# Attention on one core: q's shifted projection is turned in place of its features, and key sums and gate products are issued as four column quarters

## Chip, core and metric

One core of one Trainium2 chip. The metric is device time in microseconds (us) for one launch. The engines are TensorE (PE, with its weight loads shown apart as PEld), VectorE (DVE), ScalarE (ACT), GpSimd (POOL) and SyncE (SP), which works off its instructions beside the others; each does its own in the order in which they stand.

## The reference

Linear attention with an exponential feature map, then two top-1 mixtures of experts on its rows. Shapes: 8 batches, 8 heads, 576 rows, head dimension 64, 128 projected features; 4608 rows of 512 for the experts, 8 experts with a hidden size of 1024. The change touches the attention and the first gate alone:

```python
def phi(x):
    proj = np.einsum('bhsd,df->bhsf', x, w_phi)
    proj = proj - np.max(np.abs(proj), axis=-1, keepdims=True)
    return np.concatenate([np.exp(proj), np.exp(-proj)], axis=-1)
q_p, k_p = (phi(q), phi(k))
kv = np.einsum('bhsf,bhsd->bhfd', k_p, v)
z = np.sum(k_p, axis=2)
num = np.einsum('bhsf,bhfd->bhsd', q_p, kv)
den = np.einsum('bhsf,bhf->bhs', q_p, z)[..., None] + 1e-06
...
logits = x @ w_gate
```

A row's 256 features are thus two halves, exp(d) and exp(-d), of the same shifted projection d (128 values). `den` needs the key sums `z`; `logits` are the gate products, taken for the gate and the output gate together.

## The kernel before

The attention works through 32 heads: four groups (pairs of batches), eight heads each. A head has 2 x 576 rows in nine tiles of 128: eight whole ones and a last one that holds the 64 left-over rows of either batch. For a head the program makes the features of k and q, and in between finishes the head before it (`prev`):

- `turn` (L559) transposes k, q and the left-over tile on TensorE (L563) and splits them into high and low parts (ACT L567, DVE L568).
- `phi` (L571) makes the projection with three products per pair of tiles (L580 to L582, bank `pj`), takes the largest magnitude (DVE L584), subtracts it (DVE L585, tile `d`), and writes both halves with two exponentials (ACT L589, L590).
- `sums` (L604) forms k's features times v, one batch in either column half of the array (L611), copied to SBUF by ACT (L613). `total` (L593) adds k's features over the tiles on GpSimd into `fs` (L597 to L602).
- `turn_q` (L628) transposes q's features: 16 transposes (L635) for the eight tiles, copied by ACT and DVE in turn (L637), and two more (L640, copy L641) for the last one. The result `qt` has the features on partitions.
- `turn_sums` (L615) transposes the products (L620) and sums `fs` over its 128 partitions: four products whose weights are a 128 x 128 piece of `fs` and whose moving operand is one column of ones (L623). DVE copies both (L625, L626).
- `rows_out` (L644) multiplies `qt` with them (L653, L659, bank `nm`) and divides (L663 to L665).

After the eighth head of a group, `finish` (L669) stores the rows and makes three steps, each of which has the gate products of three tiles (`logits`, L499): per chunk of 128 features three transposes (L508), a copy (L510), and one product whose 32 columns of weights fill a quarter of the output partitions (L511, bank `lt`); a copy (L514) and a second product (L516) add the quarters. The last step also routes the 1152 rows (`route`, L111: a chain of small DVE operations, two rank products, L162 and L163, and nine scatters on GpSimd, L184). `next_part` (L709) takes one such step at two places of each following head.

```python
lt = ps.tile([P, 512], F32, tag=tag, name="lt", bufs=2)[:, :nt * P]
for kc in range(KC):
    tp = ps.tile([P, 4, P], F32, tag="tp", name="tp", bufs=3)[:, :nt, :]
    ...
    nc.tensor.matmul(lt[kc * GW:(kc + 1) * GW, :], gates[:, kc, :],
                     xt.rearrange("p t c -> p (t c)"), start=True, stop=True)
```

PSUM banks are rings: `tp` has three (all transposes), `pj` three, `nm` two (`kvt`, `kv`, `nm`, `lg`, `lt`, `rk`). In the attention the order on each engine is set by a scheduler when the program is built, not by the order of the text; the experts keep the order of the text. The experts (L307 on) run from about 546 us to the end.

Of the kernel before, what the change touches and what calls it, by code (L numbers as in the profile page):

```python
"""Linear attention with an exponential feature map, then two top-1 mixtures of experts.

Layout of the work
- Attention: per pair of batches and head, the 2 x 576 rows are nine tiles of 128 rows: four of each
  batch, and one whose halves are the last 64 rows of either batch. Scores, key sums and outputs
  stay on chip; the rows of x go to DRAM once.
- Routing: logits, first maximum, gate, and a row's rank among its expert's rows (a product with a
  strictly triangular matrix). A row's id and gate are scattered into a table [rank % 128, expert,
  rank / 128]; entries that no row takes keep the id of a row of zeros.
- Experts: an expert's weights are loaded and split once; its rows are gathered in blocks of 256 (or  # L10
  128 for a short rest), as many as its count asks for. Products run as float32r passes
  over exact high and low parts (high*high, high*low, low*high).
"""
# [17 lines left out]
P = 128  # L31
B, H, S, DH = 8, 8, 576, 64
N, D, F, E = B * S, H * DH, 1024, 8
NF = 128
# [9 lines left out]
class Fused:  # L44
# [8 lines left out]
    def consts(self):  # L53
# [5 lines left out]
        # upper[i, j] = 1 where i < j  # L59
# [7 lines left out]
        # E, E-1, .. 1: the first maximum has the largest  # L67
        self.rev = const.tile([P, E], F32, name="rev")
        nc.vector.tensor_copy(self.rev, iota_e)
        # [GW * c + e, e] = 1  # L70
# [5 lines left out]
        # the table in use; ids of the rows that wait to be routed  # L76
# [21 lines left out]
    def clear_steps(self, pool, *parts):  # L98
        """Steps that zero the rows of a routing from one on, so that others can be gathered before
        these are there."""  # L100
# [10 lines left out]
    def route(self, r, lg, nt, ids, padded=False):  # L111
        """lg: SBUF [P, nt, E or 2E] logits (and output-gate logits); ids: SBUF [P, nt] int32;
        padded: ids of N stand for no row. Returns what is left to do once PSUM for ranks is at hand:
        that in turn returns the scatters into the table."""
# [7 lines left out]
        # first maximum  # L122
# [5 lines left out]
        if padded:  # L128
            # no expert, and an address outside the table
            out = sm.tile([P, NT], F32, tag="out", name="out")[:, :nt]  # L130
            nc.vector.tensor_scalar(out, ids, float(N), float(1 << 20), op0=ALU.is_ge, op1=ALU.mult)
            nc.vector.tensor_tensor(w, w, out, op=ALU.add)
        oh = sm.tile([P, NT, E], F16, tag="oh", name="oh", bufs=3)[:, :nt, :]
        nc.vector.tensor_tensor(oh, rev, w.unsqueeze(2).to_broadcast([P, nt, E]), op=ALU.is_equal)
        # rows before, by expert
# [6 lines left out]
        # gate  # L142
# [17 lines left out]
        def place(rk):  # L160
            # rank among the expert's rows
# [12 lines left out]
            # (rank % P) * E * SLOTS + rank / P  # L174
# [15 lines left out]
    def early(self, r, psum):  # L190
        """The first expert's first block, of the rows routed so far: later rows take the blocks
        after it."""
# [12 lines left out]
    def end_route(self, r, psum):  # L205
        """Counts of rows by expert, and the table, on chip."""
# [13 lines left out]
    def start_stream(self, seq):  # L220
        """Weights of the experts of seq (w1, w2, e) in turn: loaded by chunks of 128 contraction
        rows, half an expert ahead of the split into high and low parts."""
# [17 lines left out]
    def split_steps(self, i):  # L240
        """Eight steps that leave the weights of expert i of the stream split."""
# [19 lines left out]
    def expert_buffers(self, pool):  # L261
        """Buffers of fixed place: what one branch leaves in them, another reads."""
# [17 lines left out]
    def place(self, r, e, c):  # L280
        """Table columns of rows c*256 .. (c+1)*256 of expert e: [P, 2, (id, scale)]."""
# [12 lines left out]
    def turn(self, i, k, ps, bufs=2):  # L294
        """Gathered rows i, transposed and split into x k."""
# [224 lines left out]
    def attention(self, q, k, v, w_phi, r, pool, ps, aside):  # L520
# [192 lines left out]
        for i in range(n_heads + 1):  # L713
# [16 lines left out]
            if prev:  # L730
                turn_q(prev)
            if prev:
                turn_sums(prev)
# [69 lines left out]
```

## Time and profile before

| | |
|---|---|
| median of 3 runs | 1633.69 us (1633.20 to 1636.33) |
| profiled execution, span from first to last instruction | 1630.8 us |
| between that span and the median | 2.9 us |
| TensorE busy | 1545.3 us, 95% of the span |
| VectorE, ScalarE, GpSimd busy | 48%, 38%, 26% |
| mean granted TensorE clock | 0.969 of full speed |

The profiled execution gives its span alone; what lies around it (start and end of a launch) is taken as the 2.9 us by which the median is above it. Busy time on TensorE overlaps from one product to the next, since ends are modelled. The chain of waits is therefore the better view of what a stretch costs there: its pieces follow each other without overlap.

### The profile page before, as it was taken

How to read it: one execution, taken by the hardware profiler on the slowest of the kernel's cores; microseconds unless marked ns; L12 is line 12 of the kernel's file. 1: busy time of each engine (PE TensorE's matmuls, PEld its weight loads, DVE VectorE, ACT ScalarE, POOL GpSimd, SP SyncE). 2: the span in 40 equal slices, each digit the busy share in tenths (PEclk: the TensorE clock that was granted, in tenths of full speed). 3: DMA queues.
4: the chain of work that ended last, by engine and by line, in shares of the span. 5: the costliest groups of instructions: out<-in, count | busy, mean ns of one | idle time of the engine just before them, and what ended most of it. 6: DMA issues, size and time to landing. Idle time of an engine off the chain costs nothing.

```text
span 1630.8 us, 28157 instructions
## 1 busy us (share of the span) xinstructions
PE 1545.3 (95%) x10958; PEld 1368.2 (84%) x10958; DVE 781.7 (48%) x2003; ACT 622.3 (38%) x1147; POOL 420.9 (26%) x433
## 2 busy tenths in 40 slices
PE   7999999999999989899899999998998989998997
PEld 6887897898788679798788898987998979897996
DVE  6776776676676535262545255324143244131410
ACT  5564454455454424242344244213244234131411
POOL 3332432443253321221221222214111212101100
PEclk9999899899999999999999999999999999999998
DMA  6764222123201422240433242305133344122200
GB/s 209 243 220 142 58 74 103 45 59 115 61 16 40 144 94 80 89 156 26 145 117 114 82 144 84 103 16 186 40 112 123 104 148 161 40 80 82 97 25 28
DMA packets 99089, 163.19 MB, mean 100 GB/s; under 512 B 25819, under 2 KB 62043, under 8 KB 97760
## 3 DMA queue, kind: packets, MB, share of 16 engines
q1 hardware_dynamic: 83008, 117.98, 22.1%
q0 software_dynamic: 15776, 41.52, 7.4%
q8 instruction: 146, 2.39, 0.6%
q14 instruction: 159, 1.30, 0.2%
HBM read 118.67 MB, written 42.88 MB: 99 GB/s over the span
## 4 chain that ended last, share of the span: by engine, by line
PE 59%; issue 19%; DMA 16%; POOL 2%; DVE 2%; ACT 1%; another core or an unknown queue 0%; POOLq 0%; SPq 0%; ACTq 0%
PE nm L653 7%; DMA out_dram<-y,tab 6%; DMA xg<-r_rows,tab 6%; PE kvt L611 5%; PE hp L328 5%; PE hp L330 4%; PE hp L329 4%; PE yp L353 4%; PE yp L355 4%; PE yp L354 4%; PE tp L635 3%; DMA r_table<-pay,at 3%; PE pj L580 3%; PE pj L582 2%; PE pj L581 2%
## 5 line engine op out<-in xcount | busy, mean ns | idle before, releaser
L346 DVE SCALAR_TENSOR_TENSOR hl<-hp,hh 128x512 fp32r<-128x512 f32 x148 | 102.1, 690 | 335.9 <-ACT hh L345 335.9
L345 ACT ACTIVATE hh<-hp 128x512 fp32r<-128x512 f32 x148 | 88.4, 597 | 270.0 <-PE hp L330 251.7
L359 ACT ACTIVATE y<-yp,tab 128x512 f32<-128x512 f32 x76 | 52.3, 689 | 290.3 <-PE yp L355 225.7
L184 POOL DMA_INDIRECT r_table<-pay,at x78 | 78.5, 1007 | 263.7 <-DVE at L180 222.3
L360 POOL DMA_INDIRECT out_dram<-y,tab x38 | 38.2, 1005 | 403.5 <-ACT y L359 402.0
L653 PE MATMUL nm<-kvs,qt 128*128 128x65 f32 x1024 | 123.7, 280 | 1.7 <-DVE kvs L626 1.7
L653 PEld LDWEIGHTS nm<-kvs,qt 128*128 128x128 f32 x1024 | 122.0, 198 | 3.1 <-PE tp L563 2.3
L584 DVE TENSOR_REDUCE am<-pj 128x4 f32<-128x512 f32 (+1 forms) x160 | 100.1, 633 | 43.1 <-PE pj L582 41.2
L589 ACT ACTIVATE phi<-d 128x1024 f32<-128x1024 f32 (+1 forms) x96 | 80.8, 842 | 52.4 <-DVE d L585 42.8
L597 POOL TENSOR_TENSOR fs<-phi 128x512 f32<-128x512 f32 x32 | 40.8, 1276 | 223.0 <-ACT phi L590 125.0
L580 PE MATMUL pj<-wh,th 128*128 128x256 f32 x288 | 91.5, 321 | 7.0 <-DVE pre L140 4.8
L585 DVE TENSOR_TENSOR d<-pj,am 128x512 f32<-128x512 f32 (+1 forms) x160 | 96.3, 628 | 0.3
L289 POOL DMA_INDIRECT xg<-r_rows,tab x82 | 84.5, 1030 | 38.1 <-issue 24.1
L383 DVE COPY xt<-tp 128x512 f32<-128x512 f32 x21 | 14.5, 692 | 156.2 <-PE tp L381 156.2
L360 POOL DMA_INDIRECT r_rows<-y,tab x38 | 37.6, 989 | 189.0 <-ACT y L359 179.7
L581 PE MATMUL pj<-wl,th 128*128 128x256 f32 x288 | 84.8, 297 | 0.0
L582 PE MATMUL pj<-wh,tl 128*128 128x256 f32 x288 | 83.1, 300 | 0.0
L599 POOL TENSOR_TENSOR fs<-fs,phi 128x512 f32<-128x512 f32 x64 | 81.3, 1270 | 5.0
L590 ACT ACTIVATE phi<-d 128x1024 f32<-128x1024 f32 (+1 forms) x96 | 79.8, 831 | 0.0
L580 PEld LDWEIGHTS pj<-wh,th 128*128 128x128 f32 x288 | 57.0, 198 | 17.2 <-issue 12.4
L635 PE MATMUL tp<-ident,phi 128*128 128x128 f32 x512 | 70.4, 274 | 0.1
L304 DVE TENSOR_TENSOR x<-tp,x 128x512 fp32r<-128x512 f32 x86 | 55.2, 682 | 25.4 <-ACT x L303 25.4
(294 smaller groups left out, 4759.4 us busy)
## 6 DMA issues: line engine op xcount, KB each, us to landing
raw<-in_moe_w_dram SPq DMA_DIRECT2D x128, 512.0 KB, 4.4
r_rows<-zero SPq DMA_DIRECT2D x15, 768.0 KB, 6.7
km<-in_k_dram SPq DMA_DIRECT2D x32, 256.0 KB, 2.9
qm<-in_q_dram SPq DMA_DIRECT2D x32, 256.0 KB, 3.5
vm<-in_v_dram SPq DMA_DIRECT2D x32, 256.0 KB, 3.2
r_rows<-x SPq DMA_DIRECT2D x8, 1024.0 KB, 5.5
xg<-r_rows,tab POOLq DMA_INDIRECT x82, 5.9
r_table<-pay,at POOLq DMA_INDIRECT x78, 2.2
```

Of the source, the lines that this page charges most:

```text
L289: self.nc.gpsimd.indirect_dma_start(self.xg[i][t][:, :], None, r["rows"], bass.IndirectOffsetOnAxis(ap=self.place(r, e, c)[:, t, 0:1], axi ...
L328: nc.tensor.matmul(o, w1h[kc][:, fs], x[:, kc, 0, :], start=first, stop=False)
L345: nc.scalar.activation(oh, hp, AF.Relu)
L346: nc.vector.scalar_tensor_tensor(ol, hp, 0.0, oh.bitcast(F32), op0=ALU.max, op1=ALU.subtract)
L580: nc.tensor.matmul(o, hi[:, i + j, :], wh, start=True, stop=False)
L581: nc.tensor.matmul(o, hi[:, i + j, :], wl, start=False, stop=False)
L582: nc.tensor.matmul(o, lo[:, i + j, :], wh, start=False, stop=True)
L584: nc.vector.tensor_reduce(am, pj, axis=AX.X, op=ALU.max, apply_absolute_value=True)
L585: nc.vector.tensor_tensor(d[:, 2 * i:2 * i + 2 * m, :], pj, am.unsqueeze(2).to_broadcast([P, 2 * m, NF]), op=ALU.subtract)
L611: nc.tensor.matmul(kvt[64 * b:64 * b + 64, :], v, f, start=(t == 0), stop=(t == 4))
L635: nc.tensor.transpose(tp[:, t, :], u["fq"][:, 4 * b + t, s * NF:(s + 1) * NF], self.ident)
L653: nc.tensor.matmul(nm[:, t, :], qt[:, s, 4 * b + t, :], kv[:, 2 * b + s, :], start=(s == 0), stop=(s == 1))
```

## The change

q's shifted projection `d` itself is transposed (nine transposes a head) and the two exponentials are taken by ScalarE from PSUM straight into `qt`; q's features are never written, save in the left-over tile's half for k. `key_sums` is new: four products with 32 columns of ones as weights and 128 columns of `fs` moving, each into its quarter of the partitions, a copy (`zt`) and one transpose. `logits` is parted: `turn_x` does twelve transposes with three copies 512 wide (before: four copies 384 wide), and the four gate products stand one after another. A group now leaves six steps in place of three, and `next_part` is called at three places of a head.

```diff
+    def turn_x(self, x, nt, ps, pool):
+        nc = self.nc
+        xt = pool.tile([P, KC * nt, P], F32, tag="xt", name="xt", bufs=1)
+        n = KC * nt
+        for j in range(0, n, 4):
+            tp = ps.tile([P, 4, P], F32, tag="tp", name="tp", bufs=3)
+            for i in range(j, j + 4):
+                kc, t = divmod(i, nt)
+                nc.tensor.transpose(tp[:, i - j, :], x[:, t, kc * P:(kc + 1) * P], self.ident)
+            (nc.scalar.copy if j % 8 else nc.vector.tensor_copy)(xt[:, j:j + 4, :], tp)
+        return xt
...
         for kc in range(KC):
-            tp = ps.tile([P, 4, P], F32, tag="tp", name="tp", bufs=3)[:, :nt, :]
-            for i in range(nt):
-                nc.tensor.transpose(tp[:, i, :], x[:, i, kc * P:(kc + 1) * P], self.ident)
-            xt = pool.tile([P, nt, P], F32, tag="xt", name="xt", bufs=2)
-            (nc.scalar.copy if kc % 2 else nc.vector.tensor_copy)(xt, tp)
             nc.tensor.matmul(lt[kc * GW:(kc + 1) * GW, :], gates[:, kc, :],
-                             xt.rearrange("p t c -> p (t c)"), start=True, stop=True)
+                             xt[:, kc * nt:(kc + 1) * nt, :].rearrange("p t c -> p (t c)"),
+                             start=True, stop=True)
...
-        ones = pool.tile([P, 1], F32, name="ones")
+        ones = pool.tile([P, GW], F32, name="ones")
...
-        def phi(x, n):
+        def shifted(x, n, own, tag, bufs):
             hi, lo = x
-            d = pool.tile([P, 2 * n, NF], F32, tag=f"d{n}", name=f"d{n}", bufs=2)
+            d = own.tile([P, 2 * n, NF], F32, tag=tag, name="d", bufs=bufs)
...
+            return d
+
+        def phi(d, n, tag):
+            f = self.shared.tile([P, n, 2 * NF], F32, tag=tag, name=tag, bufs=3 if n > 1 else 2)
             nc.scalar.activation(f[:, :, :NF], d, AF.Exp)
             nc.scalar.activation(f[:, :, NF:], d, AF.Exp, scale=-1.0)
...
+        def key_sums(u):
+            zp = ps.tile([P, 512], F32, tag="nm", name="zp", bufs=2)[:, :NF]
+            for b in range(2):
+                for s in range(2):
+                    i = 2 * b + s
+                    nc.tensor.matmul(zp[i * GW:(i + 1) * GW, :], ones, u["fs"][:, b, s * NF:(s + 1) * NF],
+                                     start=True, stop=True)
+            u["zt"] = pool.tile([P, NF], F32, tag="zt", name="zt", bufs=1)
+            nc.scalar.copy(u["zt"], zp)
+
         def turn_sums(u):
...
-                for b in range(2):
-                    i = 2 * b + s
-                    nc.tensor.matmul(z[:, i:i + 1], u["fs"][:, b, fs], ones, start=True, stop=True)
+            nc.tensor.transpose(kvp[:, 2 * P:3 * P], u["zt"], self.ident)
+            z = kvp[:, 2 * P:3 * P].rearrange("p (i c) -> p i c", i=4)[:, :, 0]
...
         def turn_q(u):
             qt = pool.tile([P, 2, NT, P], F32, tag="qt", name="qt", bufs=1)
-            for b in range(2):
+            for t0, n, d in ((0, 4, u["dq"]), (4, 4, u["dq"]), (8, 1, u["dh"][:, 1:2, :])):
+                tp = ps.tile([P, 4, P], F32, tag="tp", name="tp", bufs=3)[:, :n, :]
+                for t in range(n):
+                    nc.tensor.transpose(tp[:, t, :], d[:, (t0 + t) % 8, :], self.ident)
                 for s in range(2):
-                    tp = ps.tile([P, 4, P], F32, tag="tp", name="tp", bufs=3)
-                    for t in range(4):
-                        nc.tensor.transpose(
-                            tp[:, t, :], u["fq"][:, 4 * b + t, s * NF:(s + 1) * NF], self.ident)
-                    (nc.scalar.copy if s else nc.vector.tensor_copy)(qt[:, s, 4 * b:4 * b + 4, :], tp)
-            tp = ps.tile([P, 4, P], F32, tag="tp", name="tp", bufs=3)
-            for s in range(2):
-                nc.tensor.transpose(tp[:, s, :], u["fh"][:, 1, s * NF:(s + 1) * NF], self.ident)
-            nc.scalar.copy(qt[:, :, 8, :], tp[:, :2, :])
+                    nc.scalar.activation(qt[:, s, t0:t0 + n, :], tp, AF.Exp, scale=(1.0, -1.0)[s])
...
-            return [lambda i=i: part(i) for i in range(0, NT, 3)]
+            return [lambda f=f, i=i: f(i) for f, i in (
+                (turned, 0), (part, 0), (turned, 3), (part, 3), (turned, 6), (part, 6))]
...
             if u:
-                u["fk"] = phi(tk, 4)
+                u["fk"] = phi(shifted(tk, 4, pool, "dk", 1), 8, "phi4")
...
             if prev:
+                key_sums(prev)
                 turn_q(prev)
+            next_part()
             if prev:
                 turn_sums(prev)
             if u:
-                u["fq"] = phi(tq, 4)
-                u["fh"] = phi(th, 1)
+                u["dq"] = shifted(tq, 4, self.shared, "phi4", 3)
+                u["dh"] = shifted(th, 1, pool, "dh", 2)
+                u["fh"] = phi(u["dh"][:, :1, :], 1, "phi1")
```

The scheduler's order at three places. Line numbers of the change are some nine to nineteen higher: L589 to L591 are the projection, L624 `kvt`, L635 the key sums, L645 and L646 the turns of `kvt` and `zt`, L658 the turns of `d`, L660 the exponentials into `qt`, L672 and L678 the products `nm`, L519 and L525 the gate products.

TensorE in an ordinary head of the second group, from the last product of k's projection to the first of q's; before:

```order
L582 MATMUL pj<-wh,tl_2637 128x256
L635 MATMUL tp<-ident,phi_2580 128x128 x12
L620 MATMUL kv<-ident,kvt 128x128
L623 MATMUL kv<-ones,fs 128x1 x2
L620 MATMUL kv<-ident,kvt 128x128
L635 MATMUL tp<-ident,phi_2580 128x128 x4
L623 MATMUL kv<-ones,fs 128x1 x2
L580 MATMUL pj<-wh,th_2685 128x256
```

and of the change:

```order
L591 MATMUL pj<-wh,tl_2514 128x256
L635 MATMUL zp<-fs,ones 32x128 x4
L658 MATMUL tp<-ident,d 128x128 x9
L645 MATMUL kv<-ident,kvt 128x128 x2
L646 MATMUL kv<-ident,zt 128x128
L589 MATMUL pj<-wh,th_2562 128x256
```

Before, two further turns (L640) stand among q's projection; now none do. The key sums have moved ahead of the turns. Behind them both orders have q's projection (15 products), `nm`, the turns of the next head, `kvt` and k's projection; only now the tenth of the 16 `nm` products has two turns of `km` ahead of it.

ScalarE in such a head, from `kvt`'s copy on; before:

```order
L613 COPY kvt<-kvt 128x256
L637 COPY qt<-tp 128x512
L589 ACTIVATE phi_3045<-d_3024 128x8x128
L590 ACTIVATE phi_3045<-d_3024 128x8x128
L637 COPY qt<-tp 128x512
L641 COPY qt<-tp 128x2x128
```

and of the change:

```order
L626 COPY kvt<-kvt 128x256
L638 COPY zt<-zp 128x128
L660 ACTIVATE qt<-tp 128x512 x3
L602 ACTIVATE phi_2901<-d 128x8x128
L603 ACTIVATE phi_2901<-d 128x8x128
L660 ACTIVATE qt<-tp 128x512
L660 ACTIVATE qt<-tp 128x128 x2
```

k's exponentials now stand behind three of q's, and the fourth of q's behind them. The other two of q's copies before are DVE's.

TensorE in the second head after a group's end, about the gate products; before:

```order
L611 MATMUL kvt<-phi_1929,vh_121 64x256 x2
L511 MATMUL lt<-xt,r_gates 32x384 x2
L580 MATMUL pj<-wh,th_1994 128x256
L581 MATMUL pj<-wl,th_1994 128x256
L582 MATMUL pj<-wh,tl_1995 128x256
L563 MATMUL tp<-ident,qm 128x128 x3
L511 MATMUL lt<-xt,r_gates 32x384 x2
L563 MATMUL tp<-ident,qm 128x128
L563 MATMUL tp<-ident,kqh 128x128
L635 MATMUL tp<-ident,phi_1918 128x128 x3
L516 MATMUL lg<-chunk_sum,ls 128x16 x3
```

and of the change:

```order
L624 MATMUL kvt<-phi_1823,vh_121 64x256 x2
L519 MATMUL lt<-xt,r_gates 32x384 x4
L525 MATMUL lg<-chunk_sum,ls 128x16 x3
L635 MATMUL zp<-fs,ones 32x128 x4
L658 MATMUL tp<-ident,d 128x128 x9
L519 MATMUL lt<-xt,r_gates 32x384 x4
L572 MATMUL tp<-ident,km 128x128 x4
L572 MATMUL tp<-ident,qm 128x128 x4
L572 MATMUL tp<-ident,kqh 128x128
L525 MATMUL lg<-chunk_sum,ls 128x16 x3
```

The four gate products of a step now stand together; between the first of these groups and the product that reads its copy stands nothing, where before there were turns and projections. The second and third step have come together in this head.

## Rows read from the trace of the kernel before

**Rows 1.** The page: the span, and busy time of each engine.

```profile
span 1630.8 us, 28157 instructions
...
PE 1545.3 (95%) x10958; PEld 1368.2 (84%) x10958; DVE 781.7 (48%) x2003; ACT 622.3 (38%) x1147; POOL 420.9 (26%) x433
```

**Rows 2.** Windows: stretch, its us, busy PE, PEld, DVE, ACT, POOL, clock, DMA share, GB/s.

```profile
480.00:520.00 40.00, 39.76 (x360) 36.40 (x360) 30.21 (x70) 21.09 (x35) 17.82 (x17) 1.00 0.05 15
```

**Rows 3.** Chain of waits, one ordinary head: start, us, what; projection and kvt left out.

```profile
208.89 0.39 PE nm L659 x8
209.28 1.13 PE tp L563 x9
...
214.35 1.31 PE tp L635 x12
215.66 0.11 PE kv L620
215.77 0.34 PE kv L623 x4
216.11 0.17 PE kv L620
216.28 0.44 PE tp L635 x4
216.72 0.34 PE kv L623 x4
217.06 0.23 PE pj L580
...
217.88 0.22 PE tp L640 x2
...
219.17 3.52 PE nm L653 x32
222.69 0.39 PE nm L659 x8
```

**Rows 4.** Groups of instructions on ACT: line, names, shapes, count | busy us, mean ns.

```profile
L589 ACT ACTIVATE phi<-d 128x1024 f32<-128x1024 f32 x64 | 67.9, 1061 | 52.4 <-DVE d L585 42.8 <-DVE pre L140 9.6
...
L637 ACT COPY qt<-tp 128x512 f32<-128x512 f32 x64 | 37.1, 579 | 52.3 <-PE tp L635 52.3
...
L345 ACT ACTIVATE hh<-hp 128x512 fp32r<-128x512 f32 x148 | 88.4, 597 | 270.0 <-PE hp L330 251.7
```

**Rows 5.** Chain of waits: gate products, first and last piece of two groups.

```profile
135.41 0.77 PE lt L511 x4
...
163.51 0.77 PE lt L511 x4
...
528.63 1.07 PE lt L511 x4
...
542.62 2.18 PE lt L511 x6
```

**Rows 6.** Windows of 4 us where a group's rows are routed.

```profile
174.00:178.00 4.00, 2.41 (x12) 1.90 (x11) 3.78 (x16) 2.01 (x3) 0.45 (x1) 0.62 0.76 217
178.00:182.00 4.00, 4.00 (x24) 3.76 (x24) 1.13 (x9) 0.60 (x2) 0.81 (x2) 0.50 0.00 0
182.00:186.00 4.00, 4.00 (x24) 2.80 (x24) 2.52 (x6) 0.00 (x0) 2.50 (x3) 0.60 0.01 0
```

**Rows 7.** Instructions of POOL in order of time: a scatter, and the last key sums.

```profile
185.25 0.99 POOL L184 DMA_INDIRECT r_table<-pay,at  x1 [0.28 <-POOL fs L602]
186.55 0.98 POOL L184 DMA_INDIRECT r_table<-pay,at  x1 [0.30 <-issue]
...
209.79 1.52 POOL L602 TENSOR_TENSOR fs<-fs,phi 64x256 f32<-64x256 f32 x2 [1.17 <-ACT phi L590]
```

**Rows 8.** Chain of waits: a head's end, and the last gate step up to the experts.

```profile
130.87 0.39 PE nm L659 x8
...
544.82 0.49 ACT ls L514
545.36 0.85 PE lg L516 x6
546.50 0.39 PE hp L328
```

More of the change, by code (lines that the diff above doesn't have):

```diff
@@ L497, in load_gates, with logits @@
         return g, E * len(ws)
-    def logits(self, lg, x, gates, nt, ps, pool, tag):
+    def turn_x(self, x, nt, ps, pool):
[9 more added lines that the diff above has]
+        return xt
+    def logits(self, lg, xt, gates, nt, ps, pool, tag):
         nc = self.nc
@@ L587, in phi @@
                     op=ALU.subtract)
-            f = self.shared.tile([P, 2 * n, 2 * NF], F32, tag=f"phi{n}", name=f"phi{n}", bufs=3 if n > 1 else 2)
+            return d
+        def phi(d, n, tag):
+            f = self.shared.tile([P, n, 2 * NF], F32, tag=tag, name=tag, bufs=3 if n > 1 else 2)
             nc.scalar.activation(f[:, :, :NF], d, AF.Exp)
@@ L613, in sums @@
             nc.scalar.copy(u["kvt"], kvt)
+        def key_sums(u):
[7 more added lines that the diff above has]
+            nc.scalar.copy(u["zt"], zp)
         def turn_sums(u):
             kvp = ps.tile([P, 512], F32, tag="nm", name="kv", bufs=2)
-            kv, z = kvp[:, :2 * P].rearrange("p (s b d) -> p s b d", s=2, b=2), kvp[:, 2 * P:2 * P + 4]
+            kv = kvp[:, :2 * P].rearrange("p (s b d) -> p s b d", s=2, b=2)
             for s in range(2):
@@ L684, in finish, with turned @@
             lg = self.small.tile([P, NT, 2 * E], F32, tag="lgs", name="lgs", bufs=1)
+            xts = {}
+            def turned(i):
+                xts[i] = self.turn_x(x[:, i:i + 3, :], 3, ps, pool)
             def part(i):
@@ L688, in part @@
                 lgp = lgp[:, :3 * 2 * E].rearrange("p (t e) -> p t e", e=2 * E)
-                self.logits(lgp, x[:, i:i + 3, :], r["gates"], 3, ps, pool, "nm")
+                self.logits(lgp, xts.pop(i), r["gates"], 3, ps, pool, "nm")
                 nc.vector.tensor_copy(lg[:, i:i + 3, :], lgp)
```

## Prediction

> **What bounds the kernel now.** I read the busy times first: TensorE is busy 95% of the span, no other engine half of it [rows 1]. The windows then show whether that average hides a stage with another limit: in a stretch of ordinary attention heads TensorE is busy 39.76 of 40 us at full clock, VectorE 30, ScalarE 21, GpSimd 18 [rows 2]. So in an ordinary head every microsecond taken off TensorE's own stream counts, as long as nobody else becomes late. The chain of waits gives that stream piece by piece: a head takes 222.69 - 208.89 = 13.80 us, and all of its pieces are TensorE's [rows 3]. There are 32 heads. Two places are different. In the two heads after each of the first three groups, gate steps and routing are added: five heads from 130.87 to 222.69 take 91.8 us where five ordinary ones would take 69.0, so a group's steps cost 22.8 [rows 3, 8]. In them TensorE waits for the routing's chain on VectorE (2.41 of 4 us busy), after which the granted clock stands at 0.5, 1.2 GHz of 2.4, until about 185 [rows 6]: (1 - 0.62 + 1 - 0.50 + 1 - 0.60) x 4 = 5.1 us are lost to the clock per group. The last group's steps lie open between its last head and the first expert product at 546.50 [rows 8]. The experts, the other two thirds, are not touched; I carry their time over as it is.
>
> **The change, part by part.**
>
> *Turns of q.* 16 turns leave (1.31 + 0.44) and two more at 217.88 (0.22); nine come. The pieces give 0.109 us a turn, so 0.98 [rows 3]. Where a turn or float32 product is followed by a projection, the first of these takes 0.23 instead of the 0.12 that the others take; that return happens once in either order.
>
> *Key sums.* Four products with one moving column take 0.34 + 0.34 us [rows 3]. They become four of 128 columns and one turn. No row shows a product in four quarters. The nearest is a gate product: there two of them, in different quarters, share a piece of 0.77 us, 4 instructions in all, two passes each [rows 5]. With 384 columns two passes at 2.4 GHz are 0.32 + 0.32, which leaves 0.13 for changing over. At 128 columns that is 0.21 + 0.13, and I add 0.1 for entering from another form: 0.45 if all four run at once. If only two do, 0.66; if each ran alone, 4 x 0.21 + 0.23 = 1.1. I take 0.45, because the gate row shows its two products at no more than one's time.
>
> *Sum for a head.* Out: 1.75 + 0.22 + 0.68 + 0.28 (two turns of `kvt`) = 2.93, and one return of 0.11: 3.04. In: 0.45 + 0.98 + 0.39 (three turns, two at 0.11, one at 0.17 where the weights change) + 0.11 = 1.93. A head loses 1.11 us, 32 heads 35.5. Bounds with the other values of the key sums: 0.9 and 0.45.
>
> *What must keep up.* VectorE gives two 512-wide copies away. ScalarE gives two 1024-wide exponentials (1.06 each) and two copies, and takes four 512-wide exponentials from PSUM and small ones. No row has an exponential from PSUM; a copy from there is 0.58, a Relu 0.60, and the 1024-wide exponential from SBUF at 1.06 bounds it from above [rows 4]. I take 0.60, for a copy and a Relu of that very size and source agree. The price lies beside TensorE's work unless the fourth is late. The order puts it behind three others and k's two: 0.54 (four turns and the way) + 1.8 + 2.1 + 0.6 = 5.0 us after the key sums. TensorE has until then nine turns 0.98, three turns 0.39, q's projection 0.23 + 14 x 0.12 = 1.9, nine of 16 `nm` products 2.0, two turns 0.22: 5.5. It holds by half a microsecond. k's features then reach GpSimd about 1.4 later, and the key sums want them about 1.4 earlier; before, they are ready at 211.31 and read at 215.77 [rows 3, 7], so 4.4 of slack becomes some 1.6.
>
> *Gate products.* In a group after which heads follow, the chain has eight pieces like the first and last of rows 5: 6.1 us. Four together make one piece of 0.77 each of three times: 2.3. That is 3.8 for each of three groups. In the last group ten pieces (between the two rows of [rows 5], the last of these holding three) become six, since the new order has 2 + 2, 1 + 3, 1 + 3: 3.1. Together 14.5. Twelve copies fewer of `xt` in a launch are VectorE's and ScalarE's, beside this.
>
> *New waits where a group ends.* The order puts the second gate product right behind `lt`. It waits for ScalarE's copy (0.49, then the product starts 0.54 after the copy did [rows 8]) with small exponentials ahead of that copy: 1.2. The key sums share the two banks of `nm` with `lg` and wait for VectorE's copy: 0.5. Turns of the next head want `tp` banks that now each serve two exponentials: 0.9. Six scatters at 1.3 (185.25 to 186.55 [rows 7]) stand ahead of or between the next key sums, where the sums before waited behind all nine but were wanted later: up to 2.5. These add up to 5.1 a group, and one more fall of the clock would make 10. From below, a lighter VectorE could end the wait of rows 6, and with it the 5.1 of the fall: -5. I take +4, the four waits less what the half clock covers anyway. Three groups: +12.
>
> *Sum.* 1633.7 - 35.5 - 14.5 + 12 = **1595.7 us**; on the profiled span 1592.8, with 2.9 around it as now. SP's queue gets the same transfers in the same order and is not on the path.
>
> **Rivals.**
>
> *Only two quarters at once (0.10).* The rows show two gate products at a time and nothing shows three. Key sums then cost 0.21 more a head (6.7), the gate products of the first three groups two pieces a step in place of one (6.9) and the last group's two more (1.5): 1595.7 + 15.1 = 1611. The Trainium skill, "TensorEngine Tiling (Array Packing)", Tiling Modes, lists four independent tiles for 128 rows by 32 columns, which would make it one piece; the sum by that rule is the forecast. No row here has four.
>
> *The clock no longer falls (0.12).* If the waits at a group's end come spread out, the three falls go: 15.3 and the 12 of new waits less: 1568 to 1580. For it: VectorE loses two copies a head. Against: the chain that made the wait, 10 us of small operations, is all there, and there is less TensorE work to lay beside it.
>
> *More falls (0.08).* Each group end gets a second fall and the scatters' wait in full: 6 more a group, and a little more in the heads with weights to split: 1612 to 1628.
>
> *Slower: the fourth exponential of q is late (0.06).* In every ordinary head `nm` then stops at its tenth product. It decides from the 0.5 us of cover: an exponential above 0.72 us from PSUM uses it up. At the upper bound of 1.06, four cost 1.8 more and TensorE stands 1.3 us in each head: 1.3 - 1.11 = 0.2 lost, 1633.7 - 14.5 + 12 + 6 = 1637. A wait of this size is what stood before the fall in rows 6 (1.6 of 4 us), so the clock would fall too; with 5.1 lost in every second head the time is 1719. For it: ScalarE alone now empties q's turns. Against: the two rows of 0.58 and 0.60. The Trainium skill's same page, PSUM Bottleneck, says that with packed products the copies out of PSUM may bound, and advises to share these between ScalarE and VectorE, which the change gives up for q. By it this rival would be the forecast; ScalarE's 21 of 40 us [rows 2] speak against it.
>
> *Nothing to measure (0.04).* Gains and new waits cancel: this needs 16 us of waits a group.
>
> **How the numbers follow.** The forecast has 0.60, with a range of its own of 1584 to 1610. All but the last two rivals are faster: 0.60 + 0.10 + 0.12 + 0.08 = 0.90. Same 0.04, slower 0.06; 0.2%, 3 us, is about what a measurement of this kernel can tell from no change. The range runs from 1574 to 1618: it leaves out below about half of the case without falls, above the last two cases and about half of the case with more.
>
> **What would show it.** An ordinary head of 12.7 us instead of 13.80; the key sums as one piece of 0.45 in the chain, all four starting together; `lt` pieces of 0.77 that hold eight instructions; exponentials from PSUM of 0.60; TensorE still full between group ends, three stretches at half clock there; the first expert product at about 508. Heads above 13 us with a wait for `qt` or `fs` would make the forecast wrong, and so would pieces of 1.5 for four gate products.

## The result, and the profile after

| | before | changed |
|---|---|---|
| median of 4 runs | 1633.45 us (1632.15 to 1636.33) | 1596.55 us (1590.79 to 1597.70) |
| ratio | | 0.976, 95% interval 0.974 to 0.979 |
| profiled execution, span | 1630.8 us | 1596.0 us |
| first expert product | 546.50 us | 495.03 us |
| from there to the end | 1084.3 us | 1101.0 us |

The forecast was 1595.7 us, and the time is 0.9 us from it. But the last two rows say that it came so close by luck, out of two errors: the attention gained 51.5 us where 38 were forecast, and the experts, which the change does not touch, lost 16.7 where nothing was. The page of the changed kernel, the span and the busy time [rows 1]:

```profile
span 1596.0 us, 27799 instructions
...
PE 1488.2 (93%) x10702; PEld 1316.2 (82%) x10702; DVE 737.0 (46%) x1939; ACT 589.5 (37%) x1199; POOL 424.6 (27%) x433
```

The chain of waits of the changed kernel (start, us, what), with gate products of the first group, an ordinary head from key sums to key sums, and the step up to the experts [rows 3, 5, 8]:

```profile
127.44 0.78 PE lt L519 x8
...
209.74 0.35 PE zp L635 x8
210.09 1.14 PE tp L658 x9
211.22 0.22 PE kv L645 x2
211.44 0.11 PE kv L646
211.55 0.12 PE pj L589
...
213.33 1.96 PE nm L672 x18
215.29 0.23 PE tp L572 x2
215.51 1.51 PE nm L672 x14
...
222.25 0.36 PE zp L635 x8
...
493.27 1.48 PE lg L525 x6
495.03 0.58 PE hp L328
```

A head takes 222.25 - 209.74 = 12.51 us. The key sums are one piece of 0.35 with eight instructions (four products of two passes each), and the trace has the first pass of all four quarters starting within 20 ns: four at once. A gate piece of 0.78 holds eight instructions where 0.77 held four.

ScalarE in that head, in order of time (start, us, engine, instruction, in brackets its idle time before and what ended it):

```profile
210.78 1.57 ACT L660 ACTIVATE qt<-tp 128x512 f32<-128x512 f32 x3 [0.30 <-PE tp L658]
212.22 1.07 ACT L602 ACTIVATE phi<-d 128x1024 f32<-128x1024 f32 x1
213.17 1.07 ACT L603 ACTIVATE phi<-d 128x1024 f32<-128x1024 f32 x1
214.12 0.94 ACT L660 ACTIVATE qt<-tp 128x512 f32<-128x512 f32 x3
```

The fourth exponential starts at 214.12 and, at 0.6, is done by 214.7; the tenth `nm` product starts at 215.51. TensorE never waits for `qt` here.

At a group's end TensorE does wait. Windows of the changed kernel (stretch, its us, busy PE, PEld, DVE, ACT, POOL, clock, DMA share, GB/s): one wait in each of the first three groups, the stretch behind the first wait, and the last group's end, just ahead of the experts:

```profile
178.00:182.00 4.00, 1.00 (x11) 0.30 (x8) 0.00 (x0) 1.74 (x3) 2.31 (x3) 0.87 0.53 147
182.00:186.00 4.00, 4.00 (x21) 3.62 (x20) 0.51 (x3) 2.67 (x7) 3.24 (x6) 0.50 0.04 6
...
298.00:302.00 4.00, 1.42 (x14) 0.55 (x10) 0.22 (x1) 2.31 (x3) 2.10 (x3) 1.00 0.36 95
...
418.00:422.00 4.00, 2.14 (x23) 0.93 (x20) 0.54 (x2) 2.39 (x3) 3.00 (x5) 1.00 0.01 0
...
492.00:496.00 4.00, 3.06 (x13) 2.33 (x11) 1.48 (x13) 0.70 (x2) 1.45 (x2) 0.50 0.02 3
```

GpSimd ahead of the first of them, in order of time (the last row is from the ordinary head above):

```profile
172.92 0.99 POOL L184 DMA_INDIRECT r_table<-pay,at  x1 [0.15 <-issue]
173.94 1.28 POOL L612 TENSOR_TENSOR fs<-fs,phi 128x512 f32<-128x512 f32 x1
175.39 0.99 POOL L184 DMA_INDIRECT r_table<-pay,at  x1 [0.17 <-issue]
176.41 1.29 POOL L612 TENSOR_TENSOR fs<-fs,phi 128x512 f32<-128x512 f32 x1
177.86 0.99 POOL L184 DMA_INDIRECT r_table<-pay,at  x1 [0.16 <-issue]
178.89 0.73 POOL L615 TENSOR_TENSOR fs<-fs,phi 64x256 f32<-64x256 f32 x1
181.07 0.72 POOL L615 TENSOR_TENSOR fs<-fs,phi 64x256 f32<-64x256 f32 x1 [1.46 <-DMA r_table<-pay,at]
...
218.43 1.54 POOL L615 TENSOR_TENSOR fs<-fs,phi 64x256 f32<-64x256 f32 x2
```

Scatters stand between the adds, and the last add waits until they have landed. TensorE's key sums start at 181.85, and the clock stands at 0.5 (1.2 GHz of 2.4) behind that. From 30 us to the end of the attention this is TensorE's largest wait (us in total, times, longest):

```profile
PE zp L635 <- POOL fs L615: 8.7, 6, 2.5
```

The clock falls at other places than before. In the kernel before it stood at 0.5 for 10.2 us at the end of each of the first three groups, 30.7 in all. Now it does so for 6.8, 3.4 and 0 us there, and for 10.2 at the end of the last group, where it did not fall before; 6.9 of these lie ahead of the first expert product.

Now the experts. What TensorE waits for from the first expert product to the end (engine, line, cause: us in total, times, longest), before:

```profile
PE hp L328 <- issue: 26.8, 9, 7.7
```

and changed:

```profile
PE hp L328 <- issue: 37.9, 10, 7.1
```

"issue" is a wait for nothing that the profile shows as work. What it is shows one level down: an expert's short blocks are chosen by branches, and the instruction that takes the time is TensorE's own COMPARE_BRANCH. The same place in both, TensorE in order of time, with the branch that stands between the two products (its duration three times in ns, its start twice in us), before:

```profile
655.97 0.39 PE L355 MATMUL yp<-w17h,hl 128*128 128x512 f32 x1
657.00 0.36 PE L328 MATMUL hp<-x,w10h 128*128 128x256 f32 x1 [0.64 <-issue]
...
L483 PEldq COMPARE_BRANCH  x1: 237/237/237, 656.6 to 656.6; - x1
```

and changed:

```profile
603.92 0.39 PE L355 MATMUL yp<-w17h,hl 128*128 128x512 f32 x1
611.43 0.55 PE L328 MATMUL hp<-x,w10h 128*128 128x256 f32 x1 [7.12 <-issue]
...
L483 PEldq COMPARE_BRANCH  x1: 6532/6532/6532, 604.7 to 604.7; - x1
```

Each kernel makes the same 60 branches here. Before, 30 of them last over 0.5 us, 116.5 us in all; changed, 33 and 132.9. The 6th, 12th and 18th take 0.2 us before and 5.5 to 6.5 changed. TensorE's open gaps of over 1 us grow from 55.0 to 65.9 us. Its time at half clock from the first expert product on grows from 70.0 to 83.8 us (3.3 of it reach in from the attention), and half of that is lost. As an estimate the two make 10.9 + 6.9 = 17.8, for the 16.7 measured.

### The profile page after: what moved, and what is told of

Its sections match the earlier page's. It is cut to its first block, busy times and chain, and to the rows that moved or that the text cites. A ratio compares the mean times of both kernels' runs of the same rounds, so it can differ in the third digit from the quotient of the medians.

```text
span 1596.0 us, 27799 instructions
## 1 busy us (share of the span) xinstructions
PE 1488.2 (93%) x10702; PEld 1316.2 (82%) x10702; DVE 737.0 (46%) x1939; ACT 589.5 (37%) x1199; POOL 424.6 (27%) x433
## 4 chain that ended last, share of the span: by engine, by line
PE 72%; issue 12%; DMA 9%; POOL 2%; ACT 2%; DVE 2%; SPq 0%; POOLq 0%; another core or an unknown queue 0%; ACTq 0%; DVEq 0%
DMA out_dram<-y,tab 7%; PE hp L328 7%; PE hp L330 7%; PE yp L353 7%; PE yp L355 7%; PE hp L329 7%; PE yp L354 7%; PE nm L672 6%; PE kvt L624 4%; PE pj L589 2%; PE hp L333 2%; PE tp L658 2%; PE pj L591 2%; PE pj L590 2%; PE tp L301 2%
## 5 line engine op out<-in xcount | busy, mean ns | idle before, releaser
L672 PE MATMUL nm<-kvs,qt 128*128 128x65 f32 x1024 | 120.5, 273 | 3.3 <-DVE pre L140 1.5
L672 PEld LDWEIGHTS nm<-kvs,qt 128*128 128x128 f32 x1024 | 118.4, 192 | 4.9 <-issue 2.0
L589 PE MATMUL pj<-wh,th 128*128 128x256 f32 x288 | 88.3, 311 | 2.9 <-ACT th L576 1.5
L383 DVE COPY xt<-tp 128x512 f32<-128x512 f32 x21 | 14.5, 692 | 161.4 <-PE tp L381 161.4
L360 POOL DMA_INDIRECT r_rows<-y,tab x38 | 37.8, 994 | 188.7 <-ACT y L359 179.5
L660 ACT ACTIVATE qt<-tp 128x512 f32<-128x512 f32 (+1 forms) x192 | 79.5, 504 | 16.9 <-PE nm L678 8.3
L591 PE MATMUL pj<-wh,tl 128*128 128x256 f32 x288 | 82.5, 299 | 0.3
L576 ACT CAST th<-tp 128x512 fp32r<-128x512 f32 (+1 forms) x96 | 42.1, 491 | 77.9 <-PE tp L572 77.8
L328 PE MATMUL hp<-x,w10h 128*128 128x256 f32 x128 | 41.4, 324 | 27.2 <-issue 26.5
L589 PEld LDWEIGHTS pj<-wh,th 128*128 128x128 f32 x288 | 56.5, 196 | 11.0 <-ACT th L576 5.5
```

The source lines that it names most:

```text
L328: nc.tensor.matmul(o, w1h[kc][:, fs], x[:, kc, 0, :], start=first, stop=False)
L589: nc.tensor.matmul(o, hi[:, i + j, :], wh, start=True, stop=False)
L591: nc.tensor.matmul(o, lo[:, i + j, :], wh, start=False, stop=True)
L672: nc.tensor.matmul(nm[:, t, :], qt[:, s, 4 * b + t, :], kv[:, 2 * b + s, :], start=(s == 0), stop=(s == 1))
```

## The experiments

The comparisons ran at different times: the kernel before took 1633, 1663, 1633 and 1655 us in them. So totals are given as ratios to the kernel before of the same comparison, and stretches from the traces, one execution of each kernel. The three kernels with a part alone or undone ran once, and no ratio is given for them.

### Is it the place of the code that made the experts slower?

My theory was that a branch waits for instructions, and that what it costs depends on where its target lies. The trace has one instruction transfer of 16 KB for about every 256 instructions of TensorE: 34 of them while 8741 of its instructions run in the attention before, 32 for 8355 in the changed kernel. The Trainium skill, "Runtime: NRT & Kernel Launch", Instruction fetch mechanics, says the same of the blocks, and that a taken branch out of the blocks at hand waits for a transfer. The traces agree: each branch of over 0.5 us, 30 of the kernel before and 33 of the changed one, has the start of such a transfer in it, and of the shorter ones none has. 8741 is 37 over a multiple of 256, 8355 is 163 over one.

*First try: idle transposes at the start of the program,* 33 in the changed kernel, 31 in the one before.

```diff
+        for i in range(33):
+            if i % 4 == 0:
+                pad = ps.tile([P, 4, P], F32, tag="tp", name="pad", bufs=3)
+            nc.tensor.transpose(pad[:, i % 4, :], self.ident, self.ident)
```

> The changed kernel with 33 idle transposes ahead of everything on TensorE, where it waits for the first rows anyway: 132 more of its instructions ahead of the experts' code, which brings that code to the same place within blocks of 256 instructions (one instruction transfer of 16 KB each in the trace) as in the kernel before. Nothing else is changed. Theory (the experts lose 16.7 us because TensorE's branches wait for instructions, and how long depends on where the code lies): first expert product at 495 to 497 as in the changed kernel, from there to the end 1084 us as in the kernel before instead of 1101, TensorE's branches 116 us in all instead of 133; time 1580 us. Rival (the experts lose because they start earlier against their weights' transfers, or by chance): from the first product to the end 1098 to 1103, time 1596.

> The kernel before with 31 idle transposes ahead of everything on TensorE: 124 more instructions, so that the experts' code lies within its block of 256 where the changed kernel has it. Theory (place of the code): first expert product at 546 to 548, from there to the end 1101 us instead of 1084; time 1650 us. Rival (start of the experts, or chance): 1084 us to the end as before, time 1634.

Both missed. A transpose is two instructions and not four, so the code came to 229 and 99, places that neither kernel has; and the scheduler made another order of the attention, in which TensorE of the changed kernel stood still for 6.3 us in the first head, and the kernel before came to its experts at 566.1. From there to the end they took 1116.1 and 1108.6 us. Ratios 0.970 (0.965 to 0.974) and 1.010 (1.006 to 1.014). What can be read are the branches: at 229 the 3rd and 9th have become short (0.2 us, otherwise 3.0 to 3.6) and the 6th, 12th and 18th are long; at 99 those three are long too (6.5 to 7.0). The list follows the place, but no swap is shown.

*Second try: idle products between attention and experts,* 65 in the changed kernel (163 + 130 = 37 over 256), 63 in the one before (37 + 126 = 163).

```diff
+        with tc.manual_schedule():
+            pad = col("pad")
+            for _ in range(65):
+                nc.tensor.matmul(pad[:, :1], self.ones_h, self.upper[:, :1], start=True, stop=True)
         for g in range(2 * E):
```

> The changed kernel with 65 idle products of one column (130 instructions) on TensorE between the attention and the first expert, so that the attention's order is untouched and the experts' code lies where the kernel before has it: 8355 + 130 instructions stand ahead of it, 37 over a multiple of 256, as 8741 do in the kernel before. Theory (the time of a branch on TensorE depends on the place of the code alone): of the 60 branches in the experts the 6th, 12th and 18th, which take 5.5 to 6.5 us in the changed kernel, take 0.2 to 0.3 as in the kernel before; 30 branches over 0.5 us with some 116 us in all instead of 33 with 133; from the first expert product to the end about 16 us less than the changed kernel on the same chip; the products themselves cost 4 to 7 us; ratio to the kernel before 0.967 to 0.971 instead of 0.9763. Rival (chance, or the experts' earlier start): branches and experts as in the changed kernel, ratio 0.978 to 0.981.

> The kernel before with 63 such idle products (126 instructions) ahead of the first expert, so that the experts' code lies where the changed kernel has it (163 over a multiple of 256). Theory (place of the code): the 6th, 12th and 18th branch take 5.5 to 6.5 us, 33 branches over 0.5 us with some 133 us in all; 16 us more from the first expert product to the end and 4 to 7 us for the products, ratio to the kernel before 1.012 to 1.015. Rival (chance, or the experts' later start): branches as in the kernel before, ratio 1.002 to 1.005.

The branches of one line (L483, here L487) on TensorE, as minimum/median/maximum in ns. In the kernel before:

```profile
L483 PEldq COMPARE_BRANCH  x21: 67/3089/3735, 599.0 to 1596.5; - x21
```

in the changed kernel:

```profile
L483 PEldq COMPARE_BRANCH  x21: 67/3250/6532, 548.0 to 1562.8; - x21
```

in the changed kernel moved:

```profile
L487 PEldq COMPARE_BRANCH  x21: 67/3104/4010, 550.2 to 1553.9; - x21
```

and in the kernel before moved:

```profile
L487 PEldq COMPARE_BRANCH  x21: 67/3344/6184, 602.7 to 1624.2; - x21
```

The long ones went from the changed kernel to the moved one before. Over all 60: 30 long ones with 114.2 us in the changed kernel moved, 33 with 132.7 in the one before moved, and branch for branch each list of long and short ones is that of the kernel whose place it took. The wait shown above goes with it, in the changed kernel moved and in the kernel before moved:

```profile
PE hp L328 <- issue: 28.0, 9, 7.1
...
PE hp L328 <- issue: 37.9, 10, 7.4
```

The ratios are 0.970 (0.966 to 0.974) and 1.013 (1.009 to 1.018), as expected. From the first expert product to the end they take 1093.0 and 1110.6 us in that comparison: 17.6 apart, with the signs exchanged. The 65 products cost 1.87 us of TensorE, where 4 to 7 were expected. The rival of an earlier start falls, since the moved changed kernel starts its experts at 495.6 as early as the unmoved.

What the place is shown to set are the branches, and with them the open gaps: 53.5 us in the changed kernel moved, 65.1 in the one before moved. The clock's share is not fixed by it. The changed kernel moved has the branches of the kernel before, and its experts still take 1093.0 and not 1084.3, with 86.1 us at half clock for 70.0. Over all comparisons five traces at place 37 have experts of 1084.3 to 1096.4 us, four at place 163 of 1101.0 to 1116.5.

### What is each part of a head worth?

*q's part alone* on the kernel before (key sums and gate products as there):

```diff
-                u["fq"] = phi(tq, 4)
-                u["fh"] = phi(th, 1)
+                u["dq"] = shifted(tq, 4, self.shared, "phi4", 3)
+                u["dh"] = shifted(th, 1, pool, "dh", 2)
+                u["fh"] = phi(u["dh"][:, :1, :], 1, "phi1")
```

> The kernel before with q's part of the change alone: the shifted projection is turned (nine turns a head) and ScalarE takes both exponentials from PSUM; key sums and gate products as before. Theory (the turns are worth their TensorE time, the fourth exponential is covered): an ordinary head of 12.8 us instead of 13.80 (nine turns at 0.11 less), first expert product at about 514, the group ends as before with three falls of the clock. Rival (ScalarE late with q's exponentials): a head over 13.2 us with a wait for qt in it.

A head took 13.27 us: a gain of 0.53 where 1.0 was expected. Chain of waits of that kernel:

```profile
236.53 0.98 PE tp L638 x9
...
244.04 0.60 PE tp L563 x4
...
244.72 0.59 ACT th L567
```

The turns are 0.98 in place of 1.97, as costed. But TensorE now stands for 0.72 us (244.64 to 245.36) until ScalarE has made the high part of the turned rows: in this order its projection comes directly behind the turn. Neither theory had that wait. The first expert product missed by more: it came at 548.2 where 514 was expected and 546.5 stood before. The group ends took the heads' gain back, with 78.5 us at half clock in the attention for 30.7.

*Key sums alone* (`key_sums` ahead of the old `turn_q`; the buffer of `wraw` is shared with `kvt` for room):

```diff
             if prev:
+                key_sums(prev)
                 turn_q(prev)
```

> The kernel before with the key sums' part of the change alone: four products in four quarters, copy and turn, ahead of the turns of q's features; those turns, and the gate products, as before. Theory (each part is worth its own TensorE time): key sums and their turns take 0.35 + 0.13 for changing over + 0.33 instead of 0.96, so an ordinary head of 13.6 to 13.7 us instead of 13.80, and the two parts of a head (this one and q's) add up to no more than 0.7 of the 1.28 that the whole change gives: the rest comes from the order that they allow together, without TensorE's wait of 0.65 for the high parts of the turned rows that q's part alone showed. Rival (the parts add): an ordinary head of 13.05 us.

A head took 13.83 us, no gain at all. Chain of waits:

```profile
240.78 0.36 PE zp L622 x8
241.14 1.04 PE tp L646 x8
...
242.25 0.59 ACT qt L648
...
242.89 0.66 PE tp L646 x4
```

Here TensorE waits 0.7 us for a bank that ScalarE empties. The two parts alone give 0.53 - 0.03 = 0.50, both together 1.28 in the same heads. That part of the theory held, the head's time did not (13.6 to 13.7): each part alone brought a wait of about 0.7, which the joint order hides in these heads. The first expert product came at 555.2, so this part alone made the attention longer.

*The gate products undone* (q's part and key sums as changed):

> The changed kernel without its part on the gate products: three steps a group with products two at a time and four copies, next_part at two places of a head, as before; q's projection turned and key sums in quarters as changed. Theory (the gate products' part is worth what the rows of before give, 3.8 us in each of three groups and 3.1 in the last): ordinary heads of 12.52 us as in the changed kernel, first expert product at 505 to 511. Rival (the group ends are bound by the key sums on GpSimd behind the scatters and by the routing's chain, so the gate products were covered): first expert product at 493 to 498.

Heads of 12.52, first expert product at 509.9: without their part the attention is 14.8 us longer. They are worth about what they were costed at, and the rival falls. The figure is good to some 5 us: the changed kernel's own first expert product came at 495.0, 495.6 and 490.5 in three comparisons (with the idle products ahead of it in the second).

### What ends the waits at a group's end?

*Scatters queued behind the last key sum,* three a head:

```diff
-                nc.gpsimd.tensor_tensor(fs[bs, b, :], fs[bs, b, :], u["fh"][bs, 0, :], op=ALU.add)
+                self.summed = nc.gpsimd.tensor_tensor(
+                    fs[bs, b, :], fs[bs, b, :], u["fh"][bs, 0, :], op=ALU.add)
...
-                        parts.extend(scatters)
+                        def held(scatter):
+                            with self.tc.issue_after(self.summed.ins):
+                                scatter()
+                        parts.extend([lambda s=s: held(s) for s in scatters])
```

> The changed kernel with the scatters of the first three groups queued behind the last key sum of the head before, three a head, instead of nine between and ahead of the next head's key sums. Theory (TensorE's waits at group ends are for the key sums on GpSimd, which stand behind scatters and wait for these to land): the waits of 4 us in the 15th, 23rd and so on heads go, and with them the half clock that follows (6.8 and 3.4 us in the first two groups); first expert product at 478 to 484, time some 12 to 17 us under the changed kernel. Rival (the routing's chain on VectorE or ScalarE's exponentials are late there anyway): first expert product at 491 or later, time within 4 us of the changed kernel's.

The same stretch of that kernel, windows:

```profile
178.00:182.00 4.00, 3.78 (x38) 2.97 (x34) 0.25 (x1) 3.84 (x9) 3.33 (x4) 1.00 0.53 126
182.00:186.00 4.00, 3.60 (x32) 3.63 (x32) 3.51 (x10) 0.39 (x3) 2.85 (x3) 1.00 0.10 26
```

The wait and the half clock are gone in all three groups, TensorE waits for `fs` nowhere from 30 us to the end of the attention, and the first expert product is at 485.4: 9.6 earlier, just short of what was expected. That TensorE waited for the key sums behind the scatters is shown. The ratio, 0.965 (0.962 to 0.969), has no changed kernel of the same comparison beside it.

*Held and moved together,* twice, the second time beside the changed kernel itself:

> The changed kernel with both: the scatters held behind the last key sums, three a head, and 65 idle products ahead of the experts. Theory: the two gains add, since they lie in different stretches: ratio to the kernel before some 0.010 under that of the changed kernel with the idle products alone. Rival (fewer clock falls in the attention are given back in the experts): equal to it.

> The changed kernel itself, for the chip of this comparison. Every theory: first expert product at 495, branches of the experts long and short at the same places as in its first profile, with the 6th, 12th and 18th long; ratio 0.974 to 0.979.

> The kernel with the scatters held and 65 idle products ahead of the experts once more, beside the changed kernel on the same chip. Theory: 9 to 11 us from the attention and some 15 from the experts, 1.7 us for the idle products: ratio to the kernel before 0.012 to 0.016 under that of the changed kernel. Rival (most of it was the chip): less than 0.006.

First comparison: 0.9645 (0.9605 to 0.9685) against 0.9699 for moving alone, 0.005 and not 0.010; the intervals overlap, the attention's 11 us (484.6 against 495.6) are in the traces. Second: the changed kernel 0.968 (0.963 to 0.973, 1601.6 us; 0.974 to 0.979 was expected), held and moved 0.959 (0.955 to 0.963, 1586.9 us). 0.0095 is less than expected, because in this comparison the changed kernel had its first product at 490.5: the group ends cost it less than in its first profile, and the held kernel's 488.4 gains only 2.1 there; 11.2 us come from the experts (1105.6 to 1094.4). This is the fastest version found, in both comparisons.

*The gate steps at two places of a head,* over three heads, on the kernel held and moved:

```diff
-            next_part()
+            if self.placed:
+                next_part()
             if prev:
                 turn_sums(prev)
```

> The same with the six gate steps at two places of a head instead of three, so that they last three heads, while the scatters keep three places; 58 idle products, for 14 more waiting instructions of TensorE put the experts' code at the same place again. Theory (what is left at a group's end, some 14 us over five ordinary heads of which 9 are TensorE's own work, comes from three turns and two gate products crowding ScalarE and VectorE in one head): first expert product 6 to 12 us earlier than at 484.6. Rival (the routing's own chain sets it, wherever the steps stand): 482 to 487.

The opposite: first expert product at 513.9, against 488.4 for the kernel held and moved in the same comparison, and outside what either theory expected; ratio 0.974 (0.970 to 0.978). Windows:

```profile
167.00:171.00 4.00, 2.36 (x20) 1.37 (x18) 4.00 (x17) 1.62 (x5) 1.78 (x2) 1.00 0.01 2
171.00:175.00 4.00, 2.91 (x14) 2.94 (x15) 3.98 (x11) 0.51 (x2) 2.78 (x3) 0.53 0.00 0
175.00:179.00 4.00, 4.00 (x21) 4.00 (x21) 1.74 (x9) 0.00 (x0) 0.72 (x1) 0.50 0.00 0
```

VectorE is busy all of 167 to 175, with the routing's chain and the projections' maxima between its steps, while TensorE waits, and then 13.7 us at half clock follow in each group: the wait of [rows 6] again. My theory of crowding falls. From 165.2 to 172.0 the chain of waits runs over VectorE alone, so the routing's chain and the maxima are the bound there. Why the three places lay it better beside TensorE's work was not tried further.

## Why the prediction was right, and where it was not

- *Heads* were to give 32 x 1.11 = 35.5 us. Ordinary heads gained 1.33 in the first group (14.36 to 13.03), 1.28 in the next two (13.80 to 12.52) and 0.83 in the last (13.80 to 12.97): over 8, 16 and 8 heads 37.8, an estimate. The key sums cost 0.35, not 0.45, and 0.15 for changing over stands in the nine turns behind them instead (1.13 for 0.98). The projection's first product takes 0.12 in place of the returned 0.23. The rival of two quarters at once falls.
- *ScalarE's cover* held: the fourth exponential has 0.8 us to spare where half a microsecond was worked out, and the key sums are ready at 218.43 + 1.54 = 219.97 for 222.25, 2.3 of slack for the forecast 1.6. The exponential from PSUM has a median of 597 ns, as taken from copy and Relu; the rival on it falls. But the experiments on single parts show that ScalarE's place in the order can cost TensorE about 0.7 us a head, a wait that the step "what must keep up" did not look for. For the turned rows it stood in the first group's heads before and stands there still. In the changed kernel it has come new into the last group's heads, which is why these gained less. One head of the first group before, and one of the last group changed:

```profile
88.53 0.59 ACT th L567
...
455.39 0.59 ACT th L576
```

- *Gate products* were to give 14.5 us; undoing them cost 14.8.
- *New waits at group ends* were to take 12 us. Without the gate products' part the attention ends 36.6 us earlier than before, where its heads give 37.8: 1.2 were taken. This is the term that was mis-sized. The waits themselves came nearer to the forecast: TensorE's waits in the attention (from 30 us on) grew from 11.8 to 21.4 us, 9.6 where 5.1 in each of three groups was worked out, and the key sums behind the scatters are most of it. What failed is that the three falls of the clock were kept in the sum. They became shorter or went, and one came new in the last group: half clock ahead of the first expert product went from 30.7 us to 17.1, which gives some 6.8 back.
- *The experts* are the step that failed: "The experts, the other two thirds, are not touched; I carry their time over as it is". Their instructions are the same, but 386 fewer of TensorE's stand ahead of them, and three branches that took 0.2 us take about six. 16.7 us were lost: 10.9 in gaps, which follow the place of the code, and the rest at half clock, which varies at one place too.

The terms in order: -37.8 - 14.8 + 1.2 + 16.7 = -34.7, but for rounding the difference of the two spans, 34.8 (the 1.2 is what is left over, so it holds the errors of the others). Forecast were -35.5 - 14.5 + 12 + 0 = -38. Without the experts' loss the time would have been some 1580 us, 16 under the forecast; the total came close because the errors were of both signs, which is luck. The 2.9 us around the span were off too: each run on record took some 1.7 us more than its span (1597.70 for 1596.0).

## What to carry to other kernels

A stage with branches is touched by every change ahead of it on the same engine: read its branch instructions before and after, and try another place with some idle instructions (1.87 us here; the experts of the two places differed by 11 to 18 us within a comparison). Four products that fill a quarter of the partitions each cost one product's time together, if they stand one behind the other. The gain of parts measured alone need not add up: each of two parts alone made TensorE wait for ScalarE in ordinary heads, and the two together did not in half of the groups.

## What the runs showed of the hardware

- A branch on TensorE took 0.07 to 0.09 us, 0.2 to 0.4, or 3.0 to 7.8. In all fourteen traces each of the last kind has the start of a 16 KB instruction transfer in it, and none of the others has. Between the places 37 and 163, 7 of the 60 are long at one and short at the other, with the same code; five traces at 37 agree in all 60, and so do four at 163. Other engines' branches on that line stay at 0.03 to 0.06.
- Four float32 products of 32 columns of weights ran at once, both passes of all four in 0.35 us with 128 columns, and in 0.78 with 384.
- ScalarE's exponentials from PSUM follow each other every 0.49 us while each is shown with 0.59: three took 1.57.
- The kernel before took from 1633 to 1663 us over the comparisons, the changed one 1597 and 1602. Which stretch makes that difference was not profiled for the kernel before. With the same experts and the same long branches, the changed kernel's experts took 1101.0 and 1105.6 us and those with the scatters held 1116.5 (83.8, 81.6 and 97.6 us at half clock), so part of it can lie there; why stays open.
